# Splitting a Fourier stage by column parity, packing a short row tile, and moving Newton steps to GpSimd

## The chip, the core and the metric

The kernel runs on one core of a Trainium2 chip. The metric is the device time of one execution in microseconds (us); lower is better. Engines are named as in the profile: PE (TensorE), PEld (its weight loads), DVE (VectorE), ACT (ScalarE), POOL (GpSimd), SP (the queue that issues most DMAs).

## The reference, cut to what matters

A masked attention (4 batches, 8 heads, 576 rows, head size 64) writes x of 576 rows by 512 columns. A mixer then adds the real part of a two-dimensional Fourier transform to x, normalizes each row, and applies a two-layer network; a second mixer follows. This change touches the Fourier part and the normalization only:

```python
X = np.fft.fft(x, axis=1)
X = np.fft.fft(X, axis=2)
mixed = np.real(X)
u = x + mixed
un = (u - mean(u)) / np.sqrt(var(u) + 1e-06)
ch = np.maximum(un @ w_ch1, 0.0) @ w_ch2
```

All in float32. The large products are made of three products of rounded halves (high by high, high by low, low by high) in the type float32r.

## The kernel before, in words

**Order of the work.** Attention runs over 24 groups (6 for each of 4 batches), each with scores, softmax, transposes and the product with v. The Fourier transform of batch b is cut into 11 slices (three `prep`, five `s1`, three `s2`) that `fft(b)` places among the groups of the batch after the next; what is left of batch 2 runs behind the attention, and batch 3 runs inside the first steps of the network (`last_fft`). Which instruction stands where on each engine is settled by a list scheduler with its own cost model; `behind` only fixes that one instruction does not stand ahead of another.

**One batch of the Fourier part.** Rows r and -r are folded, so that 289 rows stand in three tiles of 128, 128 and 33. `prep` (L303 to L318) adds the tile `xa` to the mirrored tile `xr`, forms sums and differences of the column pairs `e` on DVE, rounds them to the high half `f` on ACT (L317) and takes the low half on POOL (L318). `s1` (L320 to L344) is the row product: for column tile mt from 0 to 3, three row tiles by three half products, 9 matmuls of 290 columns; for mt 4 (one column) 6. ACT rounds the result from PSUM to `gh` (L342), DVE subtracts to get `gl` (L344). `s2` (L346 to L376) is the column product: for each of three row tiles, 8 matmuls into `fa` and 6 into `fb`, all of 258 columns (L360). ACT copies `fa` (L364), DVE forms difference and sum `m` (L367, L368) and adds them to `xa` and `xr` (L373), and SP stores both (L375, L376). `load` (L287 to L299) brings `xa` and `xr` from DRAM with 7 DMAs for a batch; POOL clears one row in each of two tiles (L294, L296).

**Around it.** `words` (L96 to L113) unpacks weights on DVE; `slot_w` rounds them (ACT L123) and takes their low half (POOL L124). `inverse_root` (L453 to L464) is one over the root of the variance by three Newton steps of three small DVE instructions each; it runs twice, for row tiles 0 to 2 and 3 to 5. `gemm1` (L413) and `gemm2` (L432) are the products of the network; ACT (L417) and DVE (L418) make their halves `hh` and `hl`. The constants of the Fourier part are loaded at the start over POOL's queue (L538 to L542).

Of the kernel before, what the change touches and what calls it, by code (L numbers as in the profile page):

```python
# [18 lines left out]
DM = 512  # L19
# [8 lines left out]
ST = [(0, 128), (128, 128), (256, 33)]  # L28
# [15 lines left out]
def attention_fourier_mlp_kernel(ctx: ExitStack, tc: tile.TileContext, a: dict, out: bass.AP):  # L44
# [237 lines left out]
    class Fourier:  # L282
# [4 lines left out]
        def load(self, i):  # L287
            r0, n = ST[i]
# [3 lines left out]
            na = min(n, 288 - r0)  # L292
            if i == 2:
                nc.gpsimd.memset(xa[32:33], 0.0)  # L294
            if i == 0:
                nc.gpsimd.memset(xr[0:1], 0.0)  # L296
            nc.sync.dma_start(out=xa[:na], in_=xd[self.b][r0:r0 + na, :])
            for c0, c1 in ([(1, 16), (16, n)] if i == 0 else [(0, n)]):
                self.last = nc.sync.dma_start(out=xr[c0:c1], in_=xd[self.b][287 + r0 + c0:287 + r0 + c1, :])  # L299

        def prep(self, i, prev=None, prev2=None):
            r0, n = ST[i]
            f = self.f = self.k["f"]  # L303
# [4 lines left out]
            w, e = (e_pool.tile([P, DM], F32, tag=t, name=nm, bufs=nb) for t, nm in zip(tag, "we"))  # L308
            pairs = xa[:n, 1:511].rearrange("p (t c) -> p t c", t=2)
            cross = xr[:n, 1:511].rearrange("p (t c) -> p t c", t=2)[:, ::-1]  # L310
            wv = w[:n, 0:510].rearrange("p (t c) -> p t c", t=2)
            behind(nc.vector.tensor_tensor(out=wv, in0=pairs, in1=cross, op=ALU.add), prev)
            behind(nc.vector.tensor_tensor(out=e[:n, 0:512:256], in0=xa[:n, 0:512:511], in1=xr[:n, 0:512:511],
                                           op=ALU.add), prev)
            nc.vector.tensor_tensor(out=e[:n, 1:256], in0=wv[:, 0], in1=wv[:, 1], op=ALU.add)
            nc.vector.tensor_tensor(out=e[:n, 257:512], in0=wv[:, 0], in1=wv[:, 1], op=ALU.subtract)
            behind(nc.scalar.activation(out=f[:n, 0, i], in_=e[:n], func=AF.Copy), prev2)  # L317
            nc.gpsimd.tensor_tensor(out=f[:n, 1, i], in0=e[:n], in1=f32(f[:n, 0, i]), op=ALU.subtract)  # L318

        def s1(self, mt, prev=None):  # L320
            pm = ps_m("g")
            mats = []
            f = self.f
            w = self.k["ss" if mt in (2, 3) else "cs"]
            c = slice(128 * mt, 128 * mt + 128)
            m = 128 if mt < 4 else 2
# [10 lines left out]
            if mt < 4:  # L337
                gh = self.pool.tile([P, 290], F32R, tag=f"gh{mt}", name="gh", bufs=1)
                gl = self.pool.tile([P, 290], F32R, tag=f"gl{mt}", name="gl", bufs=1)
            else:  # L340
                gh, gl = self.k["g4"]
            behind(nc.scalar.activation(out=gh[:m], in_=pm[:m, :290], func=AF.Copy), self.after[0])  # L342
            self.g.append((gh, gl))
            behind(nc.vector.tensor_tensor(out=gl[:m], in0=pm[:m, :290], in1=f32(gh[:m]), op=ALU.subtract), self.after[1])  # L344

        def s2(self, i, prev=None):  # L346
            r0, n = ST[i]
            c = slice(r0, r0 + n)
            g, cd, sd, alt = self.g, self.k["cd"], self.k["sd"], self.k["alt"]

            def mats(w, gs):
                return [(l[:, c], r[:, kt]) for kt, (gh, gl) in enumerate(gs)
                        for l, r in ((gh, w[0]), (gh, w[1]), (gl, w[0]))]

            pa, pb = ps_m("fa"), ps_m("fb")
            ma = mats(cd, g[0:2]) + [(g[4][0][:, c], alt), (g[4][1][:, c], alt)]
            mb = mats(sd, g[2:4])
            for pm, mm in ((pa, ma), (pb, mb)):
                for x, (l, r) in enumerate(mm):
                    first = nc.tensor.matmul(out=pm[:n, :258], lhsT=l, rhs=r, start=x == 0, stop=x == len(mm) - 1)  # L360
                    if x == 0:
                        behind(first, prev)
            sa = self.pool.tile([P, 258], F32, tag="sa", name="sa", bufs=1)
            nc.scalar.activation(out=sa[:n, :], in_=pa[:n, :258], func=AF.Copy)  # L364
            m = self.pool.tile([P, 520], F32, tag="m", name="m", bufs=1)
            xa, xr = self.x[i]
            nc.vector.tensor_tensor(out=m[:n, 0:258], in0=sa[:n], in1=pb[:n, :258], op=ALU.subtract)  # L367
            nc.vector.tensor_tensor(out=m[:n, 258:516], in0=sa[:n], in1=pb[:n, :258], op=ALU.add)  # L368
            own = m[:n, 0:518].rearrange("p (t c) -> p t c", t=2)[:, :, 0:256]
            other = m[:n, 1:515].rearrange("p (t c) -> p t c", t=2)[:, ::-1, 0:256]  # L370
# [3 lines left out]
            na = min(n, 288 - r0)  # L374
            nc.sync.dma_start(out=ud[self.b][287 + r0:287 + r0 + n, :], in_=xr[:n])  # L375
            nc.sync.dma_start(out=ud[self.b][r0:r0 + na, :], in_=xa[:na])  # L376
# [10 lines left out]
    class Mlp:  # L387
# [52 lines left out]
        def u_tile(self, c):  # L440
            if c % 3 < 2:
                return self.lp.tile([P, DM], F32, tag="u", name="u", bufs=6)
            return self.pool.tile([P, DM], F32, tag="v", name="v", bufs=3)
# [10 lines left out]
    def inverse_root(y, var, pool):  # L454
# [35 lines left out]
    if True:  # L490
# [32 lines left out]
        cs = [fp.tile([P, 3, 290], F32R, name=f"cs{i}") for i in range(2)]  # L523
        ss = [fp.tile([P, 3, 290], F32R, name=f"ss{i}") for i in range(2)]
        cd = [fp.tile([P, 2, 258], F32R, name=f"cd{i}") for i in range(2)]
        sd = [fp.tile([P, 2, 258], F32R, name=f"sd{i}") for i in range(2)]
        alt = fp.tile([P, 258], F32R, name="alt")
        f = fp.tile([P, 2, 3, 512], F32R, name="f")
# [697 lines left out]
```

## Time and profile before

| what | value |
|---|---|
| median of 3 runs | 925.97 us (924.1 to 928.79) |
| profiled execution, its own time | 922.47 us |
| its span | 920.7 us |
| TensorE busy | 892.5 us (97%) |
| VectorE, ScalarE, GpSimd busy | 560.0, 408.3, 313.0 us |
| matmuls | 5554 |

The span is from the first to the last instruction; the profiled execution's own time has 1.8 us more around it. Matmuls are pipelined, so that a single one's duration is longer than the distance to the next; the distance is what a stream costs.

### The profile page before, as it was taken

To read this page: it belongs to the slowest core of one execution; us is meant where nothing else is said; L and a number is where in the kernel's file an instruction comes from. 1 tells how busy PE (TensorE), PEld (TensorE's weight loads), DVE (VectorE), ACT (ScalarE), POOL (GpSimd) and SP (SyncE) were. 2 spreads that over 40 slices of the span, in tenths; PEclk is the share of its full clock that TensorE was granted. 3 is DMA by queue.
4 is the path that set the end of the run, shared out by engine and by line. 5 is a ranking of instruction groups with operands and counts; after the bars stand their busy time and mean duration, and the time that the engine had idled before them with its cause. 6 is when DMAs were issued, how large, how long until landed. Compare 5 with 4: busy or idle time off the path is not lost.

```text
span 920.7 us, 15422 instructions
## 1 busy us (share of the span) xinstructions
PE 892.5 (97%) x5554; PEld 824.2 (90%) x5554; DVE 560.0 (61%) x1046; ACT 408.3 (44%) x1069; POOL 313.0 (34%) x372
## 2 busy tenths in 40 slices
PE   7989989999999999999999999999999999999997
PEld 6979988999998989998888897777899999999997
DVE  4667979798894434443443446645434444888774
ACT  5978776353442333233223224323455545444432
POOL 3122222332330133344444333422223001946660
PEclk9989999999999999999999999999999999999999
DMA  9997864234431354644744665579833287156351
GB/s 260 282 289 216 255 205 136 98 127 146 138 111 68 99 160 146 196 128 126 220 141 136 209 200 180 176 262 313 293 120 147 104 270 243 36 161 222 125 203 47
DMA packets 116972, 161.00 MB, mean 175 GB/s; under 512 B 9662, under 2 KB 70180, under 8 KB 116896
## 3 DMA queue, kind: packets, MB, share of 16 engines
q1 hardware_dynamic: 114928, 157.29, 54.0%
q0 software_dynamic: 1712, 2.51, 1.1%
q8 instruction: 44, 0.72, 0.3%
q14 instruction: 32, 0.26, 0.1%
q10 hardware_dynamic: 256, 0.21, 0.1%
HBM read 104.92 MB, written 55.06 MB: 174 GB/s over the span
## 4 chain that ended last, share of the span: by engine, by line
PE 63%; DVE 11%; DMA 9%; ACT 5%; issue 4%; POOL 4%; SPq 3%; POOLq 0%; DVEq 0%; ACTq 0%
PE oo L1036 14%; PE oo L432 10%; PE h L413 10%; PE z L895 8%; PE y L895 4%; DMA wraw<-in_w1b_dram 4%; POOL wt L147 3%; PE tu L806 3%; PE tk L784 3%; PE sc L211 2%; PE w L895 2%; SPq L101 2%; DVE wu L112 2%; DVE wu L108 2%; DVE wu L113 2%
## 5 line engine op out<-in xcount | busy, mean ns | idle before, releaser
L413 PE MATMUL h<-uT,wAh 128*128 128x384 f32 x768 | 203.1, 337 | 0.2
L413 PEld LDWEIGHTS h<-uT,wAh 128*128 128x128 f32 x768 | 139.0, 188 | 5.2 <-PE g L334 0.4
L1036 PE MATMUL oo<-wo,ht 128*128 128x256 f32 x972 | 133.7, 281 | 0.0
L413 PE MATMUL h<-uT,wAl 128*128 128x384 f32 x384 | 129.0, 336 | 0.0
L1036 PEld LDWEIGHTS oo<-wo,ht 128*128 128x128 f32 x972 | 126.5, 189 | 0.0
L432 PE MATMUL oo<-wAh,hh 128*128 128x512 f32 x288 | 113.9, 398 | 4.3 <-ACT hh L417 4.2
L432 PE MATMUL oo<-wAl,hh 128*128 128x512 f32 x288 | 113.7, 395 | 0.0
L432 PE MATMUL oo<-wAh,hl 128*128 128x512 f32 x288 | 104.4, 396 | 0.2 <-DVE hl L418 0.2
L418 DVE SCALAR_TENSOR_TENSOR hl<-h,hh 128x384 fp32r<-128x384 f32 x96 | 52.6, 552 | 76.0 <-ACT hh L417 75.8
L108 DVE TENSOR_SCALAR wu<-wu 128x512 f32<-128x512 f32 (+1 forms) x62 | 38.5, 622 | 78.2 <-ACT wu L106 73.2
L124 POOL TENSOR_TENSOR wAl<-wu,wAh 128x512 fp32r<-128x512 f32 x32 | 45.9, 1437 | 104.3 <-ACT wAh L123 104.3
L417 ACT ACTIVATE hh<-h 128x384 fp32r<-128x384 f32 x96 | 45.9, 484 | 70.4 <-PE h L413 68.9
L147 POOL TENSOR_TENSOR wt<-wu 128x128 f32<-128x128 f32 x48 | 21.1, 461 | 158.3 <-DVE wu L113 158.3
L413 PEld LDWEIGHTS h<-uT,wAl 128*128 128x128 f32 x384 | 72.1, 188 | 2.8
L432 PEld LDWEIGHTS oo<-wAh,hh 128*128 128x128 f32 x288 | 54.1, 188 | 15.6 <-ACT hh L417 6.6
L106 ACT ACTIVATE wu<-wraw 128x512 f32<-128x512 f32 (+1 forms) x62 | 41.0, 662 | 60.6 <-DMA wraw<-in_w1b_dram 46.9
L895 PE MATMUL z<-ut,wo 128*128 128x384 f32 x324 | 64.5, 338 | 1.7 <-DVE ut L863 1.7
L432 PEld LDWEIGHTS oo<-wAh,hl 128*128 128x128 f32 x288 | 53.8, 188 | 13.7 <-DVE hl L418 1.3
L432 PEld LDWEIGHTS oo<-wAl,hh 128*128 128x128 f32 x288 | 54.1, 188 | 8.9
L230 ACT ACTIVATE sm<-sc,st 96x128 f32<-96x128 f32 (+2 forms) x176 | 61.6, 373 | 0.6
L895 PEld LDWEIGHTS z<-ut,wo 128*128 128x128 f32 x324 | 56.4, 188 | 2.1 <-DVE ut L863 2.0
L211 PE MATMUL sc<-k,qz 128*96 128x128 f32 (+2 forms) x352 | 51.0, 283 | 5.3 <-DMA k<-in_kt_dram 5.3
(197 smaller groups left out, 1840.9 us busy)
## 6 DMA issues: line engine op xcount, KB each, us to landing
wo<-wsd SPq DMA_DIRECT2D x84, 256.0 KB
wsd<-wraw SPq DMA_DIRECT2D x24, 448.0 KB
wsd<-wbl SPq DMA_DIRECT2D x24, 448.0 KB
u<-u2d SPq DMA_DIRECT2D x36, 256.0 KB
hd<-hs SPq DMA_DIRECT2D x12, 768.0 KB
hw<-hd SPq DMA_DIRECT2D x36, 256.0 KB
wraw<-in_w1a_dram SPq DMA_DIRECT2D x16, 512.0 KB
wraw<-in_w2a_dram SPq DMA_DIRECT2D x16, 512.0 KB
```

Of the source, the lines that this page charges most:

```text
L106: behind(nc.scalar.activation(out=f32(u), in_=f32(high), func=AF.Abs, scale=2.0**16), relu.get("hh"))
L108: clamp = eng().tensor_scalar(f32(u), f32(u), E_MIN, E_MAX, op0=ALU.max, op1=ALU.min)
L124: nc.gpsimd.tensor_tensor(out=lo[:, :n], in0=u, in1=f32(hi[:, :n]), op=ALU.subtract)
L147: nc.gpsimd.tensor_tensor(out=o, in0=x, in1=y, op=ALU.add if plus else ALU.subtract)
L211: last = nc.tensor.matmul(out=sc[:q, j * k:(j + 1) * k], lhsT=qz[self.g][:, e, hp, qs], rhs=k_t[self.b, self.g][:, hp, ks], start=False, s ...
L230: self.exp = nc.scalar.activation(out=smv[:, j, :], in_=sc[:, j, :], func=AF.Exp, scale=SCALE, bias=st[:, 1, j:j + 1], accum_out=st[:, 2, ...
L413: nc.tensor.matmul(out=h[:, :384], lhsT=l[:, ws], rhs=r[:, kd, :], start=x == 0, stop=x == 11)
L417: relu["hh"] = nc.scalar.activation(out=hh, in_=h[:, :384], func=AF.Relu)
L418: relu["hl"] = nc.vector.scalar_tensor_tensor(out=hl, in0=h[:, :384], scalar=0.0, in1=f32(hh), op0=ALU.max, op1=ALU.subtract)
L432: nc.tensor.matmul(out=self.o[c][i], lhsT=l[:, s], rhs=r, start=first and x == 0, stop=last and x == 2)
L895: Unit.last = nc.tensor.matmul(out=bank[:, :384], lhsT=w[:, c + kd * P:c + kd * P + P], rhs=r[:, kd], start=first and x == 0, stop=x == 5, ...
L1036: nc.tensor.matmul(out=acc[G][bank][:, 256 * half:256 * half + 256], lhsT=lh[:, i], rhs=w[:, c:c + 256], start=m == 0 and x == 0 and half ...
```

## The change

Fourier, row product: columns are laid out so that `prep` gives four blocks of 128 (and one single column); the third row tile (33 rows) of the high half, its low half, and 31 rows of the high half again stand in one tile `f3`, with constants to match, so that one matmul does what three did. Between row and column product, sums and differences of two row products (`both`) separate even and odd output columns, so that the column products have 130 columns. Their halves are made on ACT and POOL. Half of the additions to x (`xr`) move from DVE to POOL. The 33-row tile is loaded and stored in 6 DMAs. The Newton steps of `inverse_root` move to POOL, in four instructions each. Constants come in 5 DMAs instead of 13.

```diff
         def load(self, i):
...
+            if i < 2:
+                r0 = 128 * i
+                rows = [(xa, 0, 1 + r0, 128), (xr, 0, 288 + r0, 128)]
+            else:
+                nc.gpsimd.memset(xa[0:1], 0.0)
+                nc.gpsimd.memset(xr[32:33], 0.0)
+                rows = [(xa, 32, 0, 1), (xa, 1, 257, 15), (xa, 16, 272, 16),
+                        (xr, 0, 575, 1), (xr, 1, 544, 15), (xr, 16, 559, 16)]
...
         def prep(self, i, prev=None, prev2=None):
...
+            behind(nc.vector.tensor_tensor(out=e4[:, 2:4, 0], in0=a4[:, 1:3, 127], in1=r4[:, 2:0:-1, 127], op=add), prev)
+            behind(nc.vector.tensor_tensor(out=e4[:, 0:2, 0], in0=a4[:, 0:4:3, 0], in1=r4[:, 0:4:3, 0], op=add), prev)
+            for t, (x, y) in enumerate(((front, back), (back, front))):
+                behind(nc.vector.tensor_tensor(out=wv[:, t], in0=a4[:, x[0], x[1]], in1=r4[:, y[0], y[1]], op=add), prev)
+            nc.vector.tensor_tensor(out=e[:n, 512:513], in0=e[:n, 256:257], in1=e[:n, 384:385], op=add)
+            nc.vector.tensor_tensor(out=e4[:, 0:2, 1:128], in0=wv[:, 0], in1=wv[:, 1], op=add)
+            nc.vector.tensor_tensor(out=e4[:, 2:4, 1:128], in0=wv[:, 0], in1=wv[:, 1], op=sub)
+            h, l = (f[:, 0, i], f[:, 1, i]) if i < 2 else (f3[0:33], f3[64:97])
+            behind(nc.scalar.activation(out=h[:, 0:513], in_=e[:n, 0:513], func=AF.Copy), prev2)
+            if i == 2:
+                behind(nc.scalar.activation(out=f3[96:128, 0:513], in_=e[0:32, 0:513], func=AF.Copy), prev2)
+            nc.gpsimd.tensor_tensor(out=l[:, 0:513], in0=e[:n, 0:513], in1=f32(h[:, 0:513]), op=sub)
 
         def s1(self, mt, prev=None):
...
-            for i in range(3):
+            for i in range(2):
+                h, l = f[:, 0, i, c], f[:, 1, i, c]
                 if mt < 4:
-                    h, l = f[:, 0, i, c], f[:, 1, i, c]
-                    mats += [(h, w[0][:, i], m), (h, w[1][:, i], m), (l, w[0][:, i], m)]
+                    mats += [(h, w[:, i], 128), (h, w[:, 2 + i], 128), (l, w[:, i], 128)]
                 else:
-                    mats += [(f[:, :, i, 256], w[0][:, i], 2), (f[:, 0, i, 256:257], w[1][:, i], 1)]
+                    mats += [(f[:, :, i, 512], w[:, i], 2), (h, w[:, 2 + i], 1)]
+            mats.append((f3[:, c], w[:, 4], 128 if mt < 4 else 1))
...
+            elif mt % 2 == 0:
+                self.half = self.pool.tile([P, 290], F32, tag="gt", name="gt", bufs=1)
+                behind(nc.scalar.activation(out=self.half, in_=pm[:, :290], func=AF.Copy), self.after[0])
             else:
...
+                for x, op in enumerate((ALU.add, ALU.subtract)):
+                    behind(nc.vector.tensor_tensor(out=both[:, x], in0=self.half, in1=pm[:, :290], op=op),
+                           self.after[1])
+                for x in range(2):
+                    behind(nc.scalar.activation(out=gh[:, x], in_=both[:, x], func=AF.Copy), self.after[0])
+                    nc.gpsimd.tensor_tensor(out=gl[:, x], in0=both[:, x], in1=f32(gh[:, x]), op=ALU.subtract)
 
         def s2(self, i, prev=None):
...
+            for pm, w, g0 in ((pa, self.k["cd"], 0), (pb, self.k["sd"], 2)):
+                for x in range(2):
+                    k = slice(130 * x, 130 * x + 130)
+                    gh, gl = g[g0 + x]
+                    mm = [(gh[:, c], w[:, 0, k]), (gh[:, c], w[:, 1, k]), (gl[:, c], w[:, 0, k])]
+                    if g0 + x == 0:
+                        mm += [(t[:, c], alt) for t in g[4]]
...
-            for x, mv in ((xa, own), (xr, other)):
-                xv = x[:n].rearrange("p (t c) -> p t c", t=2)
-                nc.vector.tensor_tensor(out=xv, in0=xv, in1=mv, op=ALU.add)
+            for x, o, y in ((xa, 0, 260), (xr, 260, 0)):
+                for c, a, w in ((0, o, 131), (256, y + 1, 129)):
+                    xv = x[:n, c:c + 256].rearrange("p (r c) -> p r c", r=2)
+                    mv = m[:n, a:a + 2 * w].rearrange("p (r c) -> p r c", r=2)[:, :, 0:128]
+                    (nc.vector if x is xa else nc.gpsimd).tensor_tensor(out=xv, in0=xv, in1=mv, op=ALU.add)
...
         for _ in range(3):
-            nc.vector.scalar_tensor_tensor(out=z, in0=y, scalar=-0.5, in1=v, op0=ALU.mult, op1=ALU.mult)
-            nc.vector.tensor_tensor(out=z, in0=z, in1=y, op=ALU.mult)
-            nc.vector.scalar_tensor_tensor(out=y, in0=z, scalar=1.5, in1=y, op0=ALU.add, op1=ALU.mult)
+            nc.gpsimd.tensor_tensor(out=z, in0=y, in1=y, op=ALU.mult)
+            nc.gpsimd.tensor_tensor(out=z, in0=z, in1=v, op=ALU.mult)
+            nc.gpsimd.tensor_scalar(z, z, -0.5, 1.5, op0=ALU.mult, op1=ALU.add)
+            nc.gpsimd.tensor_tensor(out=y, in0=y, in1=z, op=ALU.mult)
```

## Rows read from the trace of the kernel before

**Rows 1.** The page: busy time of the engines, and TensorE's granted clock.

```profile
PE 892.5 (97%) x5554; PEld 824.2 (90%) x5554; DVE 560.0 (61%) x1046; ACT 408.3 (44%) x1069; POOL 313.0 (34%) x372
...
PEclk9989999999999999999999999999999999999999
```

**Rows 2.** Busy time of each engine by stretch (count), then clock and DMA.

```profile
core 0: us, PE busy (x) PEld busy (x) DVE busy (x) ACT busy (x) POOL busy (x), PEclk, DMA share, GB/s
...
66.00:148.00 82.00, 76.19 (x663) 71.79 (x661) 69.40 (x167) 63.51 (x265) 22.36 (x17) 0.98 0.70 213
148.00:220.00 72.00, 71.91 (x422) 65.82 (x423) 64.86 (x139) 31.75 (x63) 17.09 (x12) 1.00 0.41 136
```

**Rows 3.** Waits from 55 to 225 us: total, times, longest.

```profile
POOL xa L294 <- DMA ud<-xa: 8.4, 2, 7.0
...
PE sc L211 <- DMA k<-in_kt_dram: 4.4, 1, 4.4
...
PE g L334 <- DVE gl L344: 1.8, 1, 1.8
```

**Rows 4.** Chain that ended last, in order of time: start, us, what.

```profile
52.98 6.72 DMA k<-in_kt_dram
...
95.31 0.33 DVE m L367
95.64 0.33 DVE m L368
...
97.63 0.60 DVE xa L373
98.22 0.60 DVE xr L373
...
159.41 0.88 PE ut L399 x8
...
192.63 2.42 PE g L334 x18
...
210.12 0.96 PE fa L360 x8
...
215.27 0.94 PE fa L360 x8
...
227.82 4.12 PE oo L432 x18
```

**Rows 5.** Timeline of PE near 46 and 51 us, matmuls of one mask.

```profile
46.18 0.44 PE L205 MATMUL sc<-mask_s,ident_r 108*108 108x432 f32 x1
46.45 0.92 PE L211 MATMUL sc<-k,qz 128*108 128x108 f32 x8
...
51.30 0.35 PE L205 MATMUL sc<-mask_s,ident_r 108*108 108x216 f32 x1
51.49 0.54 PE L211 MATMUL sc<-k,qz 128*108 128x108 f32 x4
```

**Rows 6.** Instructions on tile `fa`: duration min/median/max in ns.

```profile
L360 PEld LDWEIGHTS fa<-cd,gh x48: 107/189/193, 87.4 to 215.5; 128*128 128x128 f32 x32, 128*33 128x33 f32 x16
```

**Rows 7.** DVE from 50 to 220 us, groups by shape: busy, mean ns, idle.

```profile
L113 DVE SCALAR_TENSOR_TENSOR wu<-wraw,wu 128x512 int32<-128x512 int32 x17 | 15.9, 938 | 0.2
...
L312 DVE TENSOR_TENSOR w<-xa,xr 128x510 f32<-128x510 f32 x8 | 6.6, 822 | 1.2 <-DMA xr<-xd 1.2
...
L313 DVE TENSOR_TENSOR e<-xa,xr 33x2 f32<-33x2 f32 x4 | 2.6, 653 | 0.0
...
L313 DVE TENSOR_TENSOR e<-xa,xr 128x2 f32<-128x2 f32 x8 | 1.2, 155 | 1.2 <-POOL f L318 1.2
```

**Rows 8.** Single lines, 50 to 220 us: duration min/median/max in ns.

```profile
L113 DVE SCALAR_TENSOR_TENSOR wu<-wraw,wu x17: 669/692/1826, 50.1 to 213.7; 128x512 int32<-128x512 int32 x17
...
L344 DVE TENSOR_TENSOR gl<-g,gh x16: 405/449/463, 76.5 to 197.3; 128x290 fp32r<-128x290 f32 x16
```

**Rows 9.** POOL and ACT, whole run, groups by shape: busy, mean ns, idle.

```profile
L318 POOL TENSOR_TENSOR f<-e,f 128x512 fp32r<-128x512 f32 x8 | 12.1, 1509 | 43.8 <-ACT f L317 38.3 <-DVE st L227 5.5
...
L147 POOL TENSOR_TENSOR wt<-wu 128x128 f32<-128x128 f32 x48 | 21.1, 461 | 158.3 <-DVE wu L113 158.3
...
L124 POOL TENSOR_TENSOR wtl<-wu,wth 128x256 fp32r<-128x256 f32 x2 | 1.7, 834 | 1.9 <-ACT wth L123 1.9
...
L342 ACT ACTIVATE gh<-g 128x290 fp32r<-128x290 f32 x16 | 6.3, 407 | 1.6 <-PE g L334 1.6
```

**Rows 10.** Newton steps on DVE, and the queue of SP near 47 us.

```profile
L462 DVE SCALAR_TENSOR_TENSOR nr<-mv,nr x6: 147/161/163, 120.9 to 153.5; 128x3 f32<-128x3 f32 x6
...
47.42 0.80 SPq L299 DMA_DIRECT2D xr<-xd  x2
```

More of the change, by code (lines that the diff above doesn't have):

```diff
@@ L27 @@
 LW = [max(0, 96 * t - 32) for t in range(6)]
-ST = [(0, 128), (128, 128), (256, 33)]
+NR, EW = (128, 128, 33), 516
 SN = [7, 7, 6, 6, 6]
@@ L291, in load @@
             self.x[i] = xa, xr
[L292 to L299, printed above, removed]
+            x = xd[self.b]
+            if i < 2:
[6 more added lines that the diff above has]
+                        (xr, 0, 575, 1), (xr, 1, 544, 15), (xr, 16, 559, 16)]
+            for t, p0, r0, n in rows:
+                self.last = nc.sync.dma_start(out=t[p0:p0 + n], in_=x[r0:r0 + n, :])
         def prep(self, i, prev=None, prev2=None):
-            r0, n = ST[i]
-            f = self.f = self.k["f"]
+            n = NR[i]
+            f, f3 = self.k["f"]
             xa, xr = self.x[i]
@@ L307, in prep @@
                 e_pool, tag, nb = self.k["mlp"], ("v", "v"), 3
[L308 to L318, printed above, removed]
+            w, e = (e_pool.tile([P, EW], F32, tag=t, name=nm, bufs=nb) for t, nm in zip(tag, "we"))
+            wv = w[:n, 0:DM].rearrange("p (t r c) -> p t r c", t=2, r=2)[:, :, :, 1:128]
@@ new lines, in prep @@
+            a4, r4, e4 = (x[:n, 0:DM].rearrange("p (r c) -> p r c", c=128) for x in (xa, xr, e))
+            add, sub = ALU.add, ALU.subtract
+            front, back = (slice(0, 4, 3), slice(1, 128)), (slice(2, 0, -1), slice(0, 127))
+            behind(nc.vector.tensor_tensor(out=e4[:, 2:4, 0], in0=a4[:, 1:3, 127], in1=r4[:, 2:0:-1, 127], op=add), prev)
+            behind(nc.vector.tensor_tensor(out=e4[:, 0:2, 0], in0=a4[:, 0:4:3, 0], in1=r4[:, 0:4:3, 0], op=add), prev)
+            for t, (x, y) in enumerate(((front, back), (back, front))):
+                behind(nc.vector.tensor_tensor(out=wv[:, t], in0=a4[:, x[0], x[1]], in1=r4[:, y[0], y[1]], op=add), prev)
@@ new lines, in s2 @@
+        def s2(self, i, prev=None):
+            n = NR[i]
+            c = slice(128 * i, 128 * i + n)
+            g, alt = self.g, self.k["alt"]
+            pa, pb = ps_m("fa"), ps_m("fb")
+            for pm, w, g0 in ((pa, self.k["cd"], 0), (pb, self.k["sd"], 2)):
[5 more added lines that the diff above has]
+                        mm += [(t[:, c], alt) for t in g[4]]
+                    for y, (l, r) in enumerate(mm):
+                        first = nc.tensor.matmul(out=pm[:n, k], lhsT=l, rhs=r, start=y == 0, stop=y == len(mm) - 1)
+                        if x == y == 0:
+                            behind(first, prev)
+            sa = self.pool.tile([P, 260], F32, tag="sa", name="sa", bufs=1)
+            nc.scalar.activation(out=sa[:n, :], in_=pa[:n, :260], func=AF.Copy)
+            m = self.pool.tile([P, 524], F32, tag="m", name="m", bufs=1)
+            xa, xr = self.x[i]
+            for o, op in ((0, ALU.subtract), (260, ALU.add)):
+                nc.vector.tensor_tensor(out=m[:n, o:o + 260].rearrange("p (c t) -> p t c", t=2),
+                                        in0=sa[:n].rearrange("p (t c) -> p t c", t=2),
+                                        in1=pb[:n, 0:260].rearrange("p (t c) -> p t c", t=2), op=op)
+            for x, o, y in ((xa, 0, 260), (xr, 260, 0)):
[3 more added lines that the diff above has]
+                    (nc.vector if x is xa else nc.gpsimd).tensor_tensor(out=xv, in0=xv, in1=mv, op=ALU.add)
+            r0 = 128 * i
+            rows = [(xa, 0, 1 + r0, 128), (xr, 0, 288 + r0, 128)] if i < 2 else [
+                (xa, 32, 0, 1), (xa, 1, 257, 15), (xa, 16, 272, 16), (xr, 0, 575, 1), (xr, 1, 544, 15), (xr, 16, 559, 16)]
+            for t, p0, r0, k in rows:
+                nc.sync.dma_start(out=ud[self.b][r0:r0 + k, :], in_=t[p0:p0 + k])
@@ L521, in attention_fourier_mlp_kernel @@
         vlast = load_vs(0)
[L523 to L528, printed above, removed]
+        cs, ss = (fp.tile([P, 5, 290], F32R, name=nm) for nm in ("cs", "ss"))
+        cd, sd = (fp.tile([P, 2, 260], F32R, name=nm) for nm in ("cd", "sd"))
+        alt = fp.tile([P, 130], F32R, name="alt")
+        f = fp.tile([P, 2, 2, EW], F32R, name="f"), fp.tile([P, EW], F32R, name="f3")
         g4 = [fp.tile([P, 290], F32R, name=f"g4{x}") for x in "hl"]
@@ L535, in attention_fourier_mlp_kernel @@
         cons.__enter__()
-        for i in range(2):
-            for t, w in ((cs[i], a["cs"][i]), (ss[i], a["ss"][i])):
-                nc.gpsimd.dma_start(out=t[:, 0:2], in_=w[:, 0:2])
-                nc.gpsimd.dma_start(out=t[:33, 2], in_=w[:33, 2])
-            nc.gpsimd.dma_start(out=cd[i], in_=a["cd"][i])
-            nc.gpsimd.dma_start(out=sd[i], in_=a["sd"][i])
+        for t, nm in ((cs, "cs"), (ss, "ss"), (cd, "cd"), (sd, "sd")):
+            nc.gpsimd.dma_start(out=t, in_=a[nm])
         nc.gpsimd.dma_start(out=alt[:2], in_=a["alt"])
@@ L1180, in _layout @@
     for nm in ("q", "k"):
-        x = np.asarray(inp[nm]).transpose(0, 1, 3, 2).copy()
-        x[:, 4:] = x[:, :3:-1][..., np.concatenate(QS if nm == "q" else KS)]
+        x = np.asarray(inp[nm])[:, HEADS].transpose(0, 1, 3, 2).copy()
+        x[:, 4:] = x[:, 4:][..., np.concatenate(QS if nm == "q" else KS)]
         if nm == "q":
```

90 lines of the change are left out of this document (34 added, 56 removed).

## The prediction

> **What bounds the kernel now.** I first read the page: PE is busy 97% of the span, no other engine above 61%, and the granted clock is full in every slice [rows 1]. The reader is to see that work taken from PE counts, and work elsewhere only where PE waits for it. Next, by stretch, where this Fourier work lies [rows 2]: from 148 to 220 us (rest of batch 2, all of batch 3) PE is busy 71.91 of 72 us, so a matmul less is time less. From 66 to 148 us (batches 0 and 1) PE is busy 76.2 of 82, DVE 69.4 and ACT 63.5: three engines near their limits, none at it. The chain of waits says the same: up to 148 us it runs mostly over DVE, with the stores into `m` and the additions to x on it, and from there over PE alone [rows 4]. The list of waits then says where PE stands still: the longest is 4.4 us for the keys of batch 1, and for the Fourier part at most 1.8 us at a time [rows 3]. A difference of 0.5% (4.6 us) is about what a measurement of this kernel can tell from none.
>
> **Part 1, fewer row products.** Before, 4 x 9 + 6 = 42 matmuls of 290 columns for a batch; after, 4 x 7 + 5 = 33. A stream of 18 takes 2.42 us, so 0.134 us each [rows 4]. Behind 148 us lie all of batch 3 (9 fewer) and column tiles 2 to 4 of batch 2 (5 fewer): 14 x 0.134 = 1.9 us off PE's path. In front of it, 22 fewer: 2.9 us.
>
> **Part 2, 130 columns in place of 258.** The number stays 42 for a batch; 84 of them lie behind 148 us. Before, they stand 0.120 us apart (0.96 / 8) with 128 weight columns and 0.118 us (0.94 / 8) with 33 [rows 4]. No row has a float32r matmul of 130 columns. From the streams of 290 and 512 columns (0.134 and 4.12 / 18 = 0.229 us) a line gives 0.43 ns a column, 121 ns at 258, which the row bears out, and 66 ns at 130. But a matmul needs its weights: a load of 33 columns is 82 ns shorter than one of 128 [rows 6], 0.86 ns a column, and eight transposes of 128 columns on 128 weight columns stand 0.88 / 8 = 0.110 us apart [rows 4], just what 128 weight columns cost at that rate. So I take 110 ns where there are 128 weight columns (56 matmuls, 10 ns saved each, 0.6 us) and 66 ns where there are 33 (28 matmuls, 52 ns saved, 1.5 us). Bounds: 66 ns for all gives 84 x 0.053 = 4.5 us, 110 ns for all 0.8 us. That few columns might cost several passages (a loss) I exclude by the mask products: between those of 432 and of 216 columns the distance to the next matmul falls from 270 to 190 ns [rows 5], 0.37 ns a column, not a rise.
>
> The Trainium skill, "TensorE: Matmul & The Clock Gate", section "Back-to-back issue gap", gives about 81 ns for each matmul in a stream of weight loads and matmuls at 128 columns. By it the 56 would save 39 ns each and part 2 would be 3.6 us instead of 2.1; the transposes here stand at 110, so I keep that.
>
> **Part 3, DVE.** A column product's two additions to x, started 0.60 us apart, become two of half the width, which cost 0.33 us each like the stores into `m` [rows 4]: 0.53 us less, 1.6 for a batch. `prep` gains two tiny instructions (0.16 us each [rows 7], some 0.1 apart): about 0.7 us more for a batch. Between the products DVE has five instructions before and after. The nine Newton instructions go: 0.16 us each [rows 10], 1.5 to 2 us with the distances between them. So DVE has some 4.5 us less behind 148 us (two column products' batches, one `prep`, one Newton) and 3.3 less in front.
>
> **Part 4, POOL.** A batch gains four subtractions of 290 columns and six additions of 256. By the rows for 128 and 256 columns (0.46 and 0.83 us [rows 9]) these are 0.93 and 0.83 us: 8.7 us for a batch. Twelve small Newton instructions have no row; between DVE's 0.16 us [rows 10] and POOL's 0.46 us for 128 columns they are 2 to 5.5 us, and I take the lower end, since they have three elements in a row. Behind 148 us that makes some 18 us more on POOL, which is busy 17 of 72 there [rows 2]; it fits. But POOL and DVE hinder each other: L113, with two inputs in SBUF, takes 669 to 1826 ns, while L344, with one in PSUM, stays within 405 to 463 [rows 8]. Over the DVE groups that vary (L113 by 4.4 us, L312 and L313 by some 3.7 and the others by as much again [rows 7, 8]) the excess over their shortest is about 14 us, against 43 us of POOL work in the same 170 us (40 of it L124 and L318): 0.32 us of DVE for each us of POOL. So 18 us of POOL cost DVE 5.8 us: 64.9 - 4.5 + 5.8 = 66.2 us, under the 68.1 that PE will need. DVE stays covered, barely; if that cover goes, the second rival gives the price. In front, 22 us of POOL cost 7, against 3.3 saved.
>
> **Part 5, ACT, waits and queues.** ACT gains two copies of 0.41 us [rows 9] and one of some 0.6 for a batch. Behind 148 us ACT is busy 32 of 72 us, so I cost it at nothing; in front it makes 2.9 us more beside 63.5. The chain between row and column product grows from ACT, DVE to DVE, ACT, POOL, some 2 x (0.4 + 0.4 + 0.9) = 3.4 us for a pair. Behind POOL's subtraction queue the low halves of the weights; the cover is the sine product, which needs the last pair only after the cosine product and, in the network, a step of some 4 us later. Newton's longer chain is covered: the second ends at 154 us, and the transposes behind it stand at 159 with 13 us of other PE work at hand; a POOL queue that stands 7.0 us for a store [rows 3] is the sort of thing that would reach it. SP issues 3 loads and 4 stores more for a batch at 0.4 us [rows 10]. Before the keys of batch 1, issued at 52.98 us [rows 4], for which PE waits 4.4 us [rows 3], stand the loads of batch 0: three more are 1.2 us later at most, nothing at least. I take 0.6. The start (fewer memsets, 0.4 MB less of constants) I cost at nothing: PE waits there for other loads.
>
> **The sum.** -1.9 - 0.6 - 1.5 + 0.6 = -3.4 us, with the front otherwise unmoved: there PE's 5 us of savings meet a DVE that gets 4 us more and an ACT with 3 more. The profiled execution's own time, 922.5, becomes 919.1; the median of the runs is 3.5 us above it, 925.97, and becomes 922.6. The bounds of part 2 and of the keys put this case at 919 to 926.
>
> **Rivals.**
> *The front follows too.* Its chain gives back PE's part 1 and 2 for two batches (2.9 + 2.1 = 5.0 us). For it: PE is busy 93% there. Against: the chain there runs over DVE. 925.97 - 4.0 - 5.0, the keys not late, is 917.0.
>
> *DVE becomes the bound (slower).* Place: 66 to 220 us; point from which it decides: 0.43 us of DVE lost for each us of POOL, where 64.9 - 4.5 + 18 x 0.43 passes 68.1. For it: my 0.32 is a mean, single instructions lose over 1 us [rows 8], and new POOL work falls where DVE is busiest. At 0.7, DVE needs 73 us behind 148 (1 us more than now) and 81.5 of 82 in front, of which half reaches the end, 6 us: 933. The Trainium skill, "SBUF — State Buffer", section "Who interferes with whom", says that a vector instruction with two SBUF inputs and a GpSimd instruction that reads SBUF block each other for the whole instruction; the trace agrees in that L113 stretches and L344 does not, and the rule alone would put the share near 1.
>
> *Columns alone set the pace of the column products*, also with 128 weight columns: part 2 is 4.5 us, and the time 920.2. Against it stands the row of transposes.
>
> *130 columns save nothing worth having with 33 weight columns either*, 110 ns throughout: 923.9. For it: before, weight width made only 2 ns of difference.
>
> **How the numbers follow.** Forecast 0.45 (0.14 of it below 921.3, where faster begins); front follows 0.20, faster; DVE bound 0.18 (0.14 slower, above 930.6); columns alone 0.08, faster; nothing at 33 columns 0.09, no change. Faster 0.42, same 0.44, slower 0.14. The forecast case and those beside it lie in 917 to 926; the range reaches down past the front case by its own 2.5 us, to 914.5, and up to 930.5, which leaves out most of the DVE case and little else. The forecast case's own range is 919 to 926.
>
> **What would show it.** Right: matmuls fall by 36 to 5518; row products keep 0.134 us; column products stand near 110 and 66 ns; PE stays busy throughout the stretch from 148 us, and the same work there ends 3 to 4 us sooner counted from its start. Wrong: PE waiting for `gl` or `hl` between 148 and 220 us; L113 near 1.2 us in the mean; the keys of batch 1 issued past 54 us; column products at 120 ns or more.

## The result, and the profile after

The changed kernel takes 935.59 us (median of 7 runs, 932.03 to 944.39), the kernel before beside it 925.45 (7 runs, 921.06 to 928.79): ratio 1.011, interval 1.0078 to 1.0143. It is slower by 10 us, and outside the range. The profiled execution took 940.07 us, 17.6 more than that of before; its granted clock, 0.971 in the mean, is the lowest of the seven (0.971 to 0.983), so it shows the loss somewhat enlarged.

The page of the changed kernel, busy time and TensorE's granted clock, beside [rows 1]:

```profile
PE 902.4 (96%) x5518; PEld 834.4 (89%) x5518; DVE 564.0 (60%) x1064; ACT 413.8 (44%) x1081; POOL 346.8 (37%) x423
...
PEclk9889697999999999999999999999999999999999
```

There are 36 matmuls fewer, and yet PE is busy 10 us longer. The clock row says why: four of the first seven slices are now below 9, where before only the third was. The windows beside [rows 2], and six short ones (columns: window, its length, busy us and count of PE, PEld, DVE, ACT, POOL, then granted clock, DMA share, GB/s):

```profile
66.00:148.00 82.00, 76.98 (x616) 73.90 (x615) 63.70 (x165) 59.36 (x252) 35.12 (x35) 0.86 0.66 209
148.00:220.00 72.00, 67.54 (x380) 61.30 (x380) 59.07 (x138) 36.95 (x80) 35.90 (x51) 0.91 0.37 113
```

```profile
96.00:100.00 4.00, 2.39 (x16) 2.18 (x17) 3.96 (x13) 3.84 (x20) 0.34 (x1) 0.89 0.79 264
100.00:104.00 4.00, 4.00 (x22) 4.00 (x22) 2.31 (x9) 2.40 (x9) 2.05 (x3) 0.50 0.49 151
...
112.00:116.00 4.00, 4.00 (x24) 3.82 (x24) 2.94 (x5) 1.08 (x3) 1.98 (x2) 0.50 0.35 131
116.00:120.00 4.00, 4.00 (x37) 3.86 (x37) 3.61 (x8) 2.69 (x15) 1.32 (x2) 0.98 0.19 55
```

From 100 to 116 us the clock stands at 0.50 (1.2 of 2.4 GHz), and PE, though busy throughout, does 22 to 24 products in 4 us in the windows shown; in the next window, at 0.98, it does 37. What it did before the clock fell is in the timeline of PE (lines picked; the bracket is the idle time ahead of the group, and its releaser):

```profile
34.82 1.99 PE L211 MATMUL sc<-k,qz 128*96 128x128 f32 x8 [2.83 <-DMA k<-in_kt_dram]
65.76 1.99 PE L211 MATMUL sc<-k,qz 128*96 128x128 f32 x8 [3.84 <-DMA k<-in_kt_dram]
97.56 1.09 PE L253 MATMUL av<-vs,pt 126*126 126x64 f32 x8 [3.14 <-ACT pt L240]
148.15 0.97 PE L253 MATMUL av<-vs,pt 108*108 108x64 f32 x8 [1.96 <-ACT pt L240]
161.20 0.85 PE L342 MATMUL g<-cs,f 128*128 128x290 f32 x2 [2.17 <-POOL f L326]
```

Each of these five waits has a half-clock stretch near it or behind it (in windows of 4 us: 32 to 44, 64 to 72, 96 to 116, 148 to 160, 160 to 168). The kernel before has only two waits of that size behind the start, 4.36 us for keys and 1.77 us for `gl`, each with one stretch (56 to 68, 120 to 124):

```profile
59.83 1.99 PE L211 MATMUL sc<-k,qz 128*96 128x128 f32 x8 [4.36 <-DMA k<-in_kt_dram]
120.47 1.61 PE L334 MATMUL g<-cs,f 128*2 128x290 f32 x6 [1.77 <-DVE gl L344]
```

The first of the five stands ahead of all Fourier arithmetic, whose first instruction on DVE starts at 58.9 us. It is for keys of batch 0, issued at 20.24 us, which take 14.45 us to land (chain of waits: start, us, what):

```profile
20.24 14.45 DMA k<-in_kt_dram
```

The kernel before issues the same keys at 19.80 us and uses them at 31.40 without a wait. While they travel, the constants do too: `cs` and `ss` now go in one transfer of 725 KB each, where before four of 290 KB and four smaller ones did that.

So I split PE's time into three terms, summed over windows of 2 us: *work* is busy time times granted clock, *slow* is busy time minus work, *idle* is the rest. The first product of the network (`h`) and the first of the second mixer (`tk`) cut the run. The first `h` of before and after (the place is the first number behind the durations):

```profile
L413 PE MATMUL h<-uT,wAh x768: 331/336/448, 147.5 to 576.7; 128*128 128x384 f32 x192
L435 PE MATMUL h<-uT,wAh x768: 331/336/525, 161.8 to 594.5; 128*128 128x384 f32 x192
```

| profiled run | first `h` at | work | slow | idle | `h` to `tk` | work | slow | idle |
|---|---|---|---|---|---|---|---|---|
| before | 147.5 | 126.7 | 4.4 | 16.4 | 442.1 | 437.4 | 0.0 | 4.7 |
| after | 161.8 | 121.7 | 17.6 | 22.5 | 445.0 | 432.5 | 6.2 | 6.3 |

That is the whole result: work falls by 5.0 and 4.9 us, slow grows by 13.2 and 6.2, idle by 6.1 and 1.6; 17.2 of the 17.6 us. Why PE waits more with less to do was the question for the runs. Three theories at first: Newton's longer chain on POOL, POOL hindering DVE, the later keys.

### The profile page after: what moved, and what is told of

Same layout as the page of the kernel before. It is cut to its first block, busy times and chain, and to the rows that moved or that the text cites. A ratio compares the mean times of both kernels' runs of the same rounds, so it can differ in the third digit from the quotient of the medians.

```text
span 938.3 us, 15483 instructions
## 1 busy us (share of the span) xinstructions
PE 902.4 (96%) x5518; PEld 834.4 (89%) x5518; DVE 564.0 (60%) x1064; ACT 413.8 (44%) x1081; POOL 346.8 (37%) x423
## 4 chain that ended last, share of the span: by engine, by line
PE 54%; DMA 14%; DVE 12%; POOL 5%; issue 5%; SPq 5%; ACT 4%; DVEq 0%; POOLq 0%; ACTq 0%
PE oo L1053 14%; PE z L912 8%; PE oo L454 7%; PE h L435 6%; PE y L912 4%; DMA wraw<-in_w1b_dram 4%; PE sc L211 3%; POOL wt L147 3%; DMA k<-in_kt_dram 3%; SPq L101 3%; PE tk L801 3%; DVE wu L112 2%; PE tu L823 2%; PE w L912 2%; DVE wu L108 2%
## 5 line engine op out<-in xcount | busy, mean ns | idle before, releaser
L435 PE MATMUL h<-uT,wAh 128*128 128x384 f32 x768 | 206.0, 342 | 0.0
L435 PEld LDWEIGHTS h<-uT,wAh 128*128 128x128 f32 x768 | 141.4, 191 | 4.5
L454 PE MATMUL oo<-wAh,hl 128*128 128x512 f32 x288 | 106.9, 400 | 1.1 <-DVE hl L440 1.1
L124 POOL TENSOR_TENSOR wAl<-wu,wAh 128x512 fp32r<-128x512 f32 x32 | 42.3, 1326 | 83.9 <-ACT wAh L123 80.1
L211 PE MATMUL sc<-k,qz 128*96 128x128 f32 (+2 forms) x352 | 54.8, 301 | 8.1 <-DMA k<-in_kt_dram 8.0
L211 PEld LDWEIGHTS sc<-k,qz 128*96 128x96 f32 (+2 forms) x352 | 50.9, 196 | 11.9 <-issue 9.7
```

Of the source, the lines that this page charges most:

```text
L124: nc.gpsimd.tensor_tensor(out=lo[:, :n], in0=u, in1=f32(hi[:, :n]), op=ALU.subtract)
L211: last = nc.tensor.matmul(out=sc[:q, j * k:(j + 1) * k], lhsT=qz[self.g][:, e, hp, qs], rhs=k_t[self.b, self.g][:, hp, ks], start=False, s ...
L435: nc.tensor.matmul(out=h[:, :384], lhsT=l[:, ws], rhs=r[:, kd, :], start=x == 0, stop=x == 11)
L454: nc.tensor.matmul(out=self.o[c][i], lhsT=l[:, s], rhs=r, start=first and x == 0, stop=last and x == 2)
```

## Experiments

All ratios are to the kernel before, run beside it on the same chip; the interval stands behind each. Where a time is given for a trace, it is of one profiled execution.

**Parts of the change undone.** Newton back on DVE (e1), the `xr` additions back on DVE (e2), both and `gl` (e3), and the third tile's six loads put behind the next batch's keys (e4):

```diff
+behind(self.last, k_load.get((self.b + 1, 0)))   # e4, for i == 2
```

> The changed kernel, but the Newton steps stand on VectorE as before. Theory N (the Newton steps on GpSimd hold up the end of attention: ScalarE waits 1.95 us for mv, and behind it the last softmax and PE): 4 to 6 of the 10 us come back, ratio to the kernel before 1.004 to 1.007, first product of the network 4 to 6 us earlier. Theory P (the new work on GpSimd slows VectorE through the port they share): under 2 us back, ratio 1.008 or more. Theory K (the keys of batch 1 are issued 5 us later behind the loads of batch 0): nothing back, ratio 1.010.

> The changed kernel, but the additions to xr stand on VectorE (24 of the new GpSimd instructions gone, 24 more on VectorE). Theory P: VectorE loses 24 x 0.34 us but gets back the stretching of its other instructions; 2 to 4 us come back, ratio 1.007 to 1.009. Theory N: under 1 us, since the Newton steps remain, though less stands ahead of them in GpSimd's queue. Theory K: nothing.

> The changed kernel with everything that moved to GpSimd back on VectorE: Newton steps, additions to xr, low halves between the products. Theories N and P both: 6 to 9 us back, ratio 1.001 to 1.004. Theory K: 0 to 2 us back, ratio 1.008 to 1.010, the keys of batch 1 still issued past 56 us.

> The changed kernel, but the six loads of the third row tile may not stand ahead of the load of the next batch's keys in SP's queue. Theory K: the keys of batch 1 are issued near 53 us again, PE's wait near 62 us shrinks by 3 us or more and 4 to 6 us come back, ratio 1.004 to 1.007. Theories N and P: the keys come earlier but the end of attention does not, ratio 1.009 to 1.011.

Measured: e1 1.0196 (1.0165 to 1.0227), e2 1.0145 (1.01 to 1.019), e3 1.0139 (1.0108 to 1.017), e4 1.0114 (1.0074 to 1.0154). Nothing comes back; e1 is even slower than the changed kernel. In e4 the keys are issued early, as SP's timeline shows, and the first `h` still comes at 154.3 us:

```profile
51.92 0.57 SPq L177 DMA_DIRECT2D k<-in_kt_dram  x1
```

So none of the three is the main cause. (Each edit also gives the list scheduler another order; more on this below.)

**The change in two halves, Newton alone, and padding.** h_pack has the new row order, six transfers each way for the third tile, packing, and `cs` and `ss` in one transfer each; h_parity all the rest; b_newton_pool is the kernel before with Newton on POOL; a_pad is the changed kernel with two products more ahead of each group (one for the last), which the group overwrites:

```diff
+extra = 2 if mt < 4 else 1
+mats = mats[:1] * extra + mats
...
```

> The kernel before with one part of the change alone: new row order, six loads for the third tile, and its high and low halves packed into one row product (14 row products fewer); columns, Newton steps and all additions as before. Theory A (the parity split is the cost: its longer way from row products to column products and its extra DVE and ACT work in the attention stretch): this kernel is 917 to 924 us, the first network product at 146 to 150 us. Theory C (TensorE gets so little work in the attention stretch that its clock is taken to half, which slows the rest): a partial loss, 922 to 929 us, with one or two half-clock stretches between 90 and 150 us that the kernel before lacks. Theory S (any new instruction order from the list scheduler costs as much, whatever is changed): 928 to 936 us.

> The change without its packing: the parity split, 130 columns, POOL additions and Newton on POOL, but the row tiles, loads and nine row products for each block as before. Theory A (the parity split is the cost): 930 to 938 us and the first network product at 153 us or later. Theory C (the half clock through too little TensorE work): 14 more row products of the kernel before are here than in the changed kernel, so at most a few us are given back: 926 to 935 us. Theory S (any new order): 928 to 936 us, as the other half.

> The kernel before with the Newton steps of the normalisations on POOL and nothing else of the change. Theory A and theory C: the product counts and the path of the Fourier stage are as before, so 921 to 927 us and the first network product at 147 to 150 us, at most 2 us for the chain of twelve instead of nine steps. Theory S (any new order): 928 to 936 us.

> The changed kernel with two extra products ahead of each row product group (overwritten by the group that follows, so the result is unchanged), which gives TensorE back the number of row products that it had before. Theory C (the half clock is the cost): 920 to 928 us, and fewer half-clock stretches between 60 and 150 us than in the changed kernel. Theory A: TensorE has slack in front, so only the clock could change there; 936 to 942 us, the 28 extra products of 0.12 us or so behind 150 us adding 2 to 4 us. Theory S: 930 to 940 us.

Measured: h_pack 1.0088 (1.0058 to 1.0119), h_parity 1.0109 (1.0076 to 1.0143), b_newton_pool 1.0007 (0.9983 to 1.0031), a_pad 1.0096 (1.0065 to 1.0128). Each half costs about as much as the whole, and Newton nothing. The times of h_pack, h_parity and a_pad lie where theory S (any new order costs as much) put them; b_newton_pool's does not. Padding gives PE back its products: in a_pad's profiled run slow falls from 17.6 to 7.0 us and the first `h` comes at 154.8 us, though 4.1 us of work are added in front. But idle stays at 22.0 us, and the ratio is not told apart from 1.011. So the clock alone does not explain the loss, and the idle time has a cause that padding leaves.

**Order, or structure?** The list scheduler gives each variant another order. So I held every engine in the order of the kernel before (o_), by edges that add no wait. And h_pack0 and a_row0 keep row 0 in the first tile, since in the new order the first token tile needs the third tile's store; their third tile comes in pieces of 31 rows and one row.

> The packing half with row 0 kept in the first row tile (the third tile holds rows 256 to 288, and its packed product leaves out one weight row's low half, that of row 256); five loads for the third tile instead of six. Theory T (with row 0 in the third tile the first token tile of a batch can be loaded for the network only when the third tile is stored, about 12 us later than before: 117 us instead of 105): this kernel is back at 917 to 924 us, the first of these loads at 102 to 108 us. Theory S (the list scheduler's new instruction order costs it, whatever edit caused it): 926 to 936 us, also with those loads early. Theory C (less TensorE work, half clock): 924 to 932 us with half-clock stretches between 30 and 160 us.

> The whole change with row 0 kept in the first row tile in the same way (the same low half of one weight row left out). Theory T: 5 to 9 us are given back, 926 to 931 us. Theory S: 930 to 942 us, as the other variants of the changed kernel. Theory A (the parity split's longer way from row to column products): as with S, at most 3 us given back.

> The packing half with row 0 in the first tile, and every engine's instructions up to the last network product held in the order in which the kernel before has them (extra edges for the scheduler alone, no waits added). Theory S: the loss is gone and the packing's own saving is left: 915 to 922 us, first network product at 144 to 149 us. Theory C: the same order with fewer products leaves gaps, so half-clock stretches stay and the time with them: 924 to 932 us. A cost of the six or five loads themselves: 923 to 928 us.

> The whole change (parity split, packing with row 0 in the first tile, POOL additions, Newton on POOL) with every engine's instructions held in the order of the kernel before; instructions that the change adds stand right behind the ones they belong to. Theory S: 912 to 922 us, first network product at 144 to 150 us. Theory A: the chain through half tile, sum and difference, high parts and low parts is as long as before and now stands in an order made without it: 926 to 940 us, with TensorE waiting for gl or gh. Theory C: 924 to 932 us.

Measured: h_pack0 1.0205 (1.0175 to 1.0234), a_row0 1.0177 (1.0148 to 1.0206), o_pack0 1.0226 (1.0193 to 1.0258), o_row0 1.0382 (1.0354 to 1.0411). Theory T missed, and theory S held for a_row0 alone (939.57 us). With the old order the loss is no smaller for packing (o_pack0 and h_pack0 overlap) and larger for the whole change, so the new order alone is not what costs. But o_pack0 can be laid beside the kernel before instruction by instruction. PE is level with it within 0.5 us up to 55 us; then the products that wait for the keys of batch 1 start 5.7 us late. The chain of waits of o_pack0 (start, us, what), and its SP timeline and waits (total, times, longest; with held orders every line reads as that of a helper, L54 or L55):

```profile
54.99 10.38 DMA k<-in_kt_dram
```

```profile
54.99 0.57 SPq L54 DMA_DIRECT2D k<-in_kt_dram  x1
59.04 0.36 SPq L54 DMA_DIRECT2D wraw<-in_w2a_dram  x1
```

```profile
SPq L54 <- DMA xa<-xd: 4.5, 3, 3.4
SPq L54 <- DMA xr<-xd: 2.4, 2, 1.9
```

The keys are issued 2.0 us later and take 10.38 us to land instead of 6.72 [rows 4], and SP then stands for 3.5 us until a piece of the third tile has landed, though nothing behind it needs that piece. The built program says why: SP's transfers wait in turn on eight semaphores, each for the landing of the one eight places ahead. In the kernel before (a wait that stands as an instruction of its own is written with its transfer):

```
41 L299 DMA xr<-xd_69 33x512 [waits DMAHW4_49]
42 L176 DMA qz_140<-in_qt_dram 64x1152 [waits DMAHW5_49,PE_49]
43 L176 DMA qz_140<-in_qt_dram 64x1152 [waits DMAHW6_49,PE_49]
44 L177 DMA k<-in_kt_dram 128x1152 [waits DMAHW7_49]
45 L101 DMA wraw<-in_w2a_dram 128x1024 [waits DMAHW0_49,Activation_49]
```

In o_pack0 the transfer behind the keys, `wraw`, stands eight places behind the first piece of 31 rows. A transfer more is thus not only 0.4 us of SP's time, but one of eight places for as long as it takes to land. That the added transfers cost the time by these places is theory L below; its rival R is that they do not.

**Transfers alone, packing without them, parity without them.**

```diff
-nc.sync.dma_start(out=xa[:na], in_=xd[self.b][r0:r0 + na, :])
+for c0, c1 in ([(0, 1), (1, 16), (16, 32)] if i == 2 else [(0, na)]):   # o_pieces
+    nc.sync.dma_start(out=xa[c0:c1], in_=xd[self.b][r0 + c0:r0 + c1, :])
... (the like for xr and for both stores)
```

> The kernel before, in its own order, with the third tile's rows loaded and stored in six pieces each instead of two, and nothing else. Theory L: 930 to 945 us, keys of the second batch issued 1.5 to 6 us later, SyncE waiting for transfers of the pieces, first network product at 155 us or later. Rival R: 921 to 926 us.

> Packing alone, with the row tiles, loads and stores of the kernel before (the packed product leaves out the low half of weight row 256) and every engine's order as before. Theory L: no transfer is added, so the front is as before or better: 916 to 923 us, keys of the second batch issued at 51 to 54 us, first network product at 144 to 149 us. Rival R: 930 to 946 us, as o_pack0.

> The same packing with the transfers of the kernel before, in the scheduler's own order. Theory L: 916 to 925 us. Rival R: 928 to 943 us. If o_ppack is near 920 and this one 5 us or more above it, the scheduler's order is a second cost.

> The parity split, POOL additions and Newton on POOL with the row tiles, loads and stores of the kernel before, every engine in the order of the kernel before. If theory L is the only cost of the change: 915 to 923 us. If the parity split has its own cost (chain through half tile, sum and difference, high and low parts; more DVE, ACT and POOL work while TensorE waits): 928 to 942 us, with TensorE waiting for gl, g4h or g4l, and keys of the second batch on time.

Measured: o_pieces 1.0059 (1.0028 to 1.0089), o_ppack 1.0027 (0.9996 to 1.0059), p_pack 1.0051 (1.0027 to 1.0076), o_parity 1.0189 (1.0154 to 1.0224). The pieces alone slow the kernel before by 0.6%, at the low end of what theory L expected. o_ppack (928.0 us) lies between theory L and its rival, p_pack (932.7) in the rival's range, so the transfers are not the only cost. The chain of o_pieces shows the keys issued 1.7 us later and landing as fast as before, unlike with o_pack0's pieces of 31 rows:

```profile
54.65 6.77 DMA k<-in_kt_dram
```

The later keys are no mark of the pieces: o_ppack, which adds no transfer, issues them at 54.52 us. The larger part stands further on. PE waits 5.09 us for `gl`, where the kernel before waits 1.77, since DVE stands for a load of `u` that follows the third tile's stores (PE's timeline, then the chain, of o_pieces):

```profile
125.52 1.61 PE L54 MATMUL g<-cs,f 128*2 128x290 f32 x6 [5.09 <-DVE gl L54]
```

```profile
114.13 2.48 DMA ud<-xa
...
116.66 4.87 DMA u<-ud
...
125.10 0.37 DVE gl L54
```

Against o_pack0, o_ppack differs in the pieces and the place of one row, and 2.0 of the 2.3% are gone. Its first network product:

```profile
L55 PE MATMUL h<-uT,wAh x768: 331/336/686, 148.0 to 580.8; 128*128 128x384 f32 x192
```

This run shows what packing is worth in front: the same order, the same transfers, 2.6 us less work before the first `h` (124.1), 3.6 us more idle (20.0), and the first `h` at 148.0 instead of 147.5. Of the idle time, 1.4 us is a longer wait for the later keys; the rest is about what the work fell by. In that order PE did not set the pace there, and work taken from it became waiting. o_parity, which adds no transfer, is far slower: DVE, held in an order made for another `prep`, waits for POOL to free `e`, which the new `prep` writes first (DVE's waits, 30 to 225 us; 1.2 us once in the kernel before [rows 7]):

```profile
DVE e L55 <- POOL f L55: 11.0, 5, 3.1
```

In the scheduler's own order (h_parity) that wait is gone and 1.1% is left.

**The chain alone, and the whole change without added transfers.** b_chain gives the kernel before the changed kernel's way from row to column products (in short form):

```diff
+elif mt % 2 == 0:
+    self.half = ...; ACT: half = pm
+else:
+    DVE: both[0] = 0 * pm + half; both[1] = 0 * half + pm
+    ACT: gh[x] = both[x]; POOL: gl[x] = both[x] - gh[x]
```

> The kernel before with the way of the changed kernel from row products to column products and nothing else: the even block copied by ACT, two DVE instructions when the odd block is there, two ACT copies, two POOL subtractions (values are passed on unchanged; the low halves of the row products come out as zero, so the column products multiply as many columns but with zeros there). Nine row products, 258 columns, transfers and Newton steps as before. Theory A (this chain is the parity split's cost): 927 to 936 us, first network product at 150 us or later, keys of the second batch on time. Rival (the chain is covered; the cost lies in the seven additions ahead of the row products or in POOL's work): 920 to 926 us.

> The whole change with the row tiles, loads and stores of the kernel before: third tile in two transfers each way, its packed product without the low half of weight row 256. Theory L (added transfers cost 5 us of the 10): 928 to 934 us, keys of the second batch issued at 51 to 55 us. If the transfers cost nothing here because other waits cover them: 934 to 940 us. If packing and parity then both cost nothing: 915 to 923 us.

Measured: b_chain 0.9963 (0.994 to 0.9986), 919.85 us against 924.18; p_all 1.0084 (1.0068 to 1.01). The longer chain costs nothing there; b_chain is even faster than both kernels. Its page and PE timeline (lines picked):

```profile
PEclk9999999999999999999999999999999999999999
```

```profile
58.87 1.30 PE L211 MATMUL sc<-k,qz 128*96 128x128 f32 x8 [3.94 <-DMA k<-in_kt_dram]
142.10 0.54 PE L334 MATMUL g<-cs,f 128*128 128x290 f32 x2 [1.10 <-DVE uT L412]
```

Behind the start these are its only waits over 1 us, one half-clock stretch follows (60 to 64 us, 0.62), and the first `h` comes at 142.5 us (work 127.8, slow 1.6, idle 13.1). Since its low halves are zero it is a measurement, not a version to use; why it is faster than the kernel before was not settled. p_all (932.61 us) lies in theory L's range, but its interval overlaps the whole change's, so the removal of the added transfers is not shown to help there.

The terms of eleven profiled runs up to the first `h`, by the same sums:

| kernel | first `h` at | work | slow | idle |
|---|---|---|---|---|
| b_chain | 142.5 | 127.8 | 1.6 | 13.1 |
| b_newton_pool | 144.7 | 127.2 | 2.6 | 14.9 |
| before | 147.5 | 126.7 | 4.4 | 16.4 |
| o_ppack | 148.0 | 124.1 | 3.9 | 20.0 |
| h_parity | 153.1 | 123.8 | 7.8 | 21.6 |
| o_pieces | 153.8 | 126.6 | 4.9 | 22.3 |
| h_pack | 154.5 | 123.5 | 8.0 | 23.0 |
| a_pad | 154.8 | 125.8 | 7.0 | 22.0 |
| p_all | 156.1 | 121.6 | 11.2 | 23.3 |
| after | 161.8 | 121.7 | 17.6 | 22.5 |
| o_pack0 | 163.5 | 124.0 | 6.9 | 32.6 |

Every kernel with less work in front than the kernel before has its first `h` later, and so it is in the nine runs left out; o_pieces, with the same work, has it later too. These are single executions.

## Why the prediction was wrong

*Part 1 and part 2 held.* 5518 matmuls, as said. Row products keep their distance: seven take 1.09 us, of which the last one's own 0.3, so 0.13 us each. Column products stand 0.11 us apart with 128 weight columns and 0.06 with 33, against 110 and 66 ns forecast (PE timeline of the changed kernel):

```profile
209.23 1.09 PE L342 MATMUL g<-ss,f 128*128 128x290 f32 x7
```

```profile
137.31 0.27 PE L378 MATMUL fa<-alt,g4h 128*128 128x130 f32 x1
137.42 0.27 PE L378 MATMUL fa<-alt,g4l 128*128 128x130 f32 x1
137.53 0.39 PE L378 MATMUL fa<-cd,gh 128*128 128x130 f32 x2
...
141.40 0.22 PE L378 MATMUL fa<-alt,g4h 128*33 128x130 f32 x1
141.46 0.23 PE L378 MATMUL fa<-alt,g4l 128*33 128x130 f32 x1
141.52 0.28 PE L378 MATMUL fa<-cd,gh 128*33 128x130 f32 x2
```

The transposes were the right row. The 81 ns that the Trainium skill, "TensorE: Matmul & The Clock Gate", section "Back-to-back issue gap", gives for 128 columns are not reached here. Work from the first `h` to the last `fb` fell by 3.6 us (68.8 to 65.2), where 4.0 were forecast.

*"With the front otherwise unmoved" is the step that failed.* The prediction let PE's 5 us of savings in front vanish, and stopped there. In the profiled runs the front moved by 14.3 us the wrong way: work did fall by 5.0, but idle time on PE grew by 6.1, and time lost in stretches at 1.2 GHz by 13.2. In these the same products take about twice as long: eight score products take 1.99 us at 65.76 us, and 1.04 at 96.16 us in the kernel before. [rows 1] showed the beginning of it in its third slice, an 8; the prediction called every slice full, and priced a wait at its length alone.

*The start, costed at nothing,* is part of that step. In the profiled run its wait is 2.8 us, with some 3 us of slow behind it. PE waits 0.75 to 3.25 us at that place in eight of the fourteen kernels that load `cs` and `ss` in one transfer each, and in none of the six that load them in parts. No run changed the constants alone, so this stays an untried cause.

*"PE stays busy throughout the stretch from 148 us, and the same work there ends 3 to 4 us sooner counted from its start"* was wrong for the same reason: from the first `h` to the last `fb` it took 69.4 us (161.8 to 231.2) against 69.0, with 2.8 us of slow and 1.2 us more idle in place of the 3.6 us saved. (The other 3.4 us of slow in the table come later.)

*The keys, +0.6 within 0 to 1.2:* mis-sized. They were issued at 58.35 us, 5.4 later [rows 4], in this run; a_pad, with the same transfers, issued them at 53.02. By e4 their lateness is not the main cost. The price was taken as issue time; a transfer is also a place among eight, and by o_pieces the added transfers alone cost the kernel before 0.6% (0.28 to 0.89), more than the whole gain forecast; in its trace more of that stands behind the stores (3.3 us) than at the keys (1.6).

*Part 4, contention:* the forecast feared too much. L113 took 0.938 us in the mean [rows 7] and now takes less, though POOL works 34 us more (DVE, groups by shape, 50 to 234 us):

```profile
L113 DVE SCALAR_TENSOR_TENSOR wu<-wraw,wu 128x512 int32<-128x512 int32 x17 | 12.9, 760 | 0.2
L393 DVE TENSOR_TENSOR xa<-xa,m 128x256 f32<-128x256 f32 x16 | 11.5, 745 | 0.0
```

The new instructions do take longer than part 3 priced them: the `xa` additions, forecast at 0.33 us, take 0.745 here and 0.481 in e3 over the same stretch, where DVE makes the `xr` additions too:

```profile
L393 DVE TENSOR_TENSOR xa<-xa,m 128x256 f32<-128x256 f32 x16 | 7.7, 481 | 0.0
```

The slower rival had the right sign and the wrong mechanism: DVE is busy 59 of 72 us from 148 to 220 us, and no run that took work off POOL gave time back. The Trainium skill, "SBUF — State Buffer", section "Who interferes with whom", has an exclusive lock on the port pair that VectorE and GpSimd share. The share near 1 that the prediction worked out from it is not seen in L113.

*Part 5, chain and Newton at nothing:* right, by b_chain and b_newton_pool, both tried in the kernel before.

*What stays open:* why the parity split alone (h_parity, no added transfers) has 5 us more idle in front. Its trace says where: 1.4 us more at the keys of batch 1 (5.73 us), and 3.4 us for `x`, which stands on DVE behind the additions of a `prep` whose first one waits for its rows (DVE, then PE):

```profile
88.03 0.16 DVE L314 TENSOR_TENSOR e<-xa,xr 128x2 f32<-128x2 f32 x1 [5.66 <-DMA xr<-xd]
```

```profile
90.84 1.10 PE L239 MATMUL tp<-ident_r,sm 126*126 126x126 f32 x4 [3.38 <-DVE x L265]
```

In the kernel before that wait of DVE is 0.74 us, at 85.31 us. What in the split brings it about was not tried. The chain, Newton, and POOL's additions are each excluded only in other settings; the seven additions of `prep` and the mere loss of products were not tried alone. That the half clock follows from the waits is argued from where its stretches lie; a_pad moved the clock and hardly the time.

## What to carry to other kernels

Read the granted clock beside every wait of TensorE: in a stretch where other engines or transfers set the pace, work taken from TensorE may buy nothing (o_ppack), and idle time can cost twice, once by its length and once by the half clock that stood near it here. Count an added transfer as a place in its queue until it lands, not as its issue time alone, and look at what else travels beside a transfer that is made larger. And split TensorE's time into work, slow and idle before and after: the work term tells whether the arithmetic of a forecast was right, the others where the time went.

## What the runs showed of the hardware

The 66 runs of the kernel before that stood beside these kernels, on five chips, had a mean granted clock from 0.987 to 0.998; a line through them loses 0.74 us for each 0.001 (correlation -0.65; 0.32 to 0.93 us by chip). The changed kernel's mean is 0.978 against 0.993. Carried on that far, outside its points, the line gives an estimate of 11 us, about what it lost; this is a correlation and not a cause.

Behind row pieces of 31 the keys of batch 1 took longer to land: 10.38 us in o_pack0, 9.47 in h_pack0, 9.19 in o_row0 and 8.37 in a_row0, the four kernels with pieces of 31 rows and one row. In the sixteen others it was 5.9 to 7.5 us, also with pieces of 1, 15 and 16 or 17 rows. What in the transfer does it was not tried alone.
